# A transformer block with sliding-window attention on one core: another order for a batch's score products, the fifth block's projection in the attention's tail, and new tables of places

## The chip, the core and the metric

The kernel runs on one core of a Trainium2 chip. A core has a matrix engine (TensorE, PE in the profile; its weight loads are PEld), VectorE (DVE), ScalarE (ACT), GpSimd (POOL) and SyncE (SP, which here only issues DMAs). Each works through its own queue in order and waits for the others on semaphores. The metric is device time in microseconds (us).

## The reference

One transformer block over 2048 rows of 640, modulated by a vector c: layer norm, attention with 32 heads of 20 in which each row sees itself and the 255 rows before it, an output projection and a gated residual; then layer norm again and an MLP of width 1536.

```python
def A(x, wqkv, wo):                       # 32 heads of 20, W = 256
    q, k, v = split(x @ wqkv)
    scores = einsum("bhqd,bhkd->bhqk", q, k) * 20 ** -0.5
    mask = (i - j >= 0) & (i - j < 256)
    p = softmax(where(mask, scores, -1e9))
    return merge(einsum("bhqk,bhkd->bhqd", p, v)) @ wo

sa, ca, ga, sb, cb, gb = silu(c) @ w_mod  # six vectors of 640
h = layernorm(x) * (1 + ca) + sa
x = x + ga * A(h, wqkv, wo)
h = layernorm(x) * (1 + cb) + sb
x = x + gb * (gelu(layernorm(h) @ w1 + b1) @ w2 + b2)
```

## The kernel before

**Precision.** Every large product is made of three: an fp32 operand is split into a high part (a cast to fp32r) and a low part (the rest), and high x high, low x high and high x low are summed in PSUM. The names end in `hi` and `lo`. A cast of the high part is mostly ACT's; the low part, a subtraction, is DVE's or POOL's.

**Stages.** A prologue normalizes the first two chunks of 512 rows and makes the first q and k. Attention then runs in 139 steps (`t`). After it comes the MLP: four chunks of 512 rows, in each twelve slices `f` of the hidden width, with fifteen products into `h` and fifteen into `out` for each.

**The order is written out.** Every instruction goes through a helper (line 119, so that all rows of the profile bear L119) that keeps each engine's instructions in the program's order. What stands where is set by tables of numbers at the top of the file:

- The prologue is a string, `ORDER`, decoded letter by letter: R a warm run of small products, T a transposed column block of the normalized rows turned in, L its low part (on POOL if its name is in `LOWP`, else DVE), P the products with it, M a column of the modulation, S statistics, N the normalization, C, E, Y the layout of q and k. `RUN0` is the length of the first warm run.
- A step t of attention issues one batch of score products, the mask and exp of one item, the row maxima of another, and the sums with v of a third; behind them stand other tasks, at quarter steps, in `plan`. The q, k and v projections ("units") are laid into the steps up to `LAST` = 108 by `lay_units`, with a room of products for each step, corrected by `EXTRA`, `EARLY`, `AFTER`, `V_COST`, `X_COST` and others.
- The second half of the block is done for 16 blocks of 128 rows by `mid_steps(bg)`: load the sums `ob`, their scale `r` and the rows `xb`; scale them (`om`, on POOL), cast (`oh`, on ACT), subtract (`ol`, on POOL); thirty products with the output projection in two halves of 320 columns (`w00` to `w04`, `w10` to `w14`, three products each), both into one PSUM bank; an add and statistics for each half (DVE); the norm (`n1`, ACT), the modulation (`m0`, `m1`), transposes of the residual (`x0`, `x1`), the second norm (`n2`) and its transposes (`y0`, `y1`). Blocks 0 to 3 run in the last steps of attention, from the times `TAIL0` and with the offsets `TAIL_AT`. Of block 4 the loads and the scaling are there too; its other steps and blocks 5 to 15 (`mids`) are spread over the MLP by `fill()`, each chunk between `lo` and `hi`.

**A batch of score products.** `score_batch` issues the products of up to two groups: e (scores with k as rows, for exp; from step 11 on) and s (scores with q as rows, for the row maxima; until step 127). Each group holds four heads, two on PE's rows 0 to 63 and two on rows 64 to 127, and its scores lie in three PSUM banks of 512 columns. Letters name the products: `a` is the part of the first half that lies in the bank which both halves share, `b` and `c` the rest of the first half; `d`, `e` and `f` the same for the second half. A digit ahead of it is the group (0 for e, 1 for s). Since both halves must not write one bank at once, an empty instruction with a wait stands ahead of the second half's product into a shared bank. Each group has one set of banks, so that e of a step waits until exp has read the e before, and s until the maximum has read the s before.

Of the kernel before, what the change touches and what calls it, by code (L numbers as in the profile page):

```python
# [10 lines left out]
F32R = mybir.dt.float32r  # L11
# [21 lines left out]
RUN0 = 33  # L33
# [8 lines left out]
UNITS = (  # L42
    (0, "q1", "k1", "v0", "v1", "q2", "k2", "v2", "q3", "k3", "v30", "q40", "k40", "v40", "q41", "k41", "v31", "v41"),
    (1, "q00", "k00", "q10", "k10", "q01", "k01", "q11", "k11", "v0", "v1", "q2", "k2", "q3", "k3", "v2", "v3", "q4", "k4", "v4"),
)
FAST = 10
LNS = [-10.5, -3.5, -1.5, -1.5, 1.75, -1.0, 0.0]
LOV = [0, 1, 3, 4, 6, 7, 12, 17, 18, 21, 23, 24, 25, 26, 29, 40, 41, 42, 43, 46, 49, 50, 53, 56, 58, 60]
HIA = [0, 2, 6, 7, 9]
MV = [8, 9, 11, 12, 15, 19, 20, 21, 23, 27, 28]  # L50
# [10 lines left out]
EXTRA = {9: -2, 10: -2, 11: 6, 12: 1, 13: -1, 14: -2, 16: -4, 18: -3, 20: -5, 21: 4, 22: 6, 23: 3, 24: 1, 25: 4, 26: -1, 27: 5, 28: -4, 29: 1, 30: -4, 33: 4, 34: -3, 35: 2, 36: 3, 37: 3, 38: -6, 40: -2, 41: -1, 42: -3, 43: -3, 44: -7, 46: 2, 51: 1, 52: -8, 53: 6, 54: -8, 55: 2, 56: -3, 59: 8, 60: -2, 61: -1, 63: -1, 64: -4, 65: 3, 66: -4, 67: -2, 68: -2, 69: -2, 70: 1, 71: 3, 72: 4, 75: -1, 76: -2, 77: -3, 78: -2, 79: -3, 80: -3, 81: -9, 82: 16, 83: 6, 84: -2, 85: -1, 86: 2, 87: -2, 88: 3, 90: 2, 91: 1, 92: 3, 93: -7, 94: -10, 96: 8, 97: 1, 98: -1, 99: 5, 102: -2, 103: 6, 104: -4, 105: -2, 106: -1, 107: -2, 108: 1, 109: 1, 110: 3, 111: 7, 112: -1, 114: -1}  # L61

EARLY = {3: (5, 0, 0), 5: (3, 0, 0), 6: (3, 0, 0), 7: (3, 0, 0), 12: (1, 0, 0), 13: (0, 0, 0), 14: (0, 0, 0), 15: (5, 0, 0), 16: (5, 0, 0), 17: (4, 0, 0), 19: (4, 0, 0), 24: (4, 0, 0), 29: (3, 0, 0), 30: (5, 0, 0), 31: (2, 0, 0), 32: (0, 0, 0), 33: (3, 0, 0), 35: (5, 0, 0), 37: (5, 0, 0), 39: (4, 0, 0), 40: (4, 0, 0), 41: (3, 0, 0), 42: (4, 0, 0), 44: (2, 0, 0), 45: (0, 0, 0), 47: (5, 0, 0)}

AFTER = {2: 2, 3: 2, 4: 3, 5: 1, 6: 1, 7: 1, 9: 1, 10: 2, 11: 1, 12: 2, 14: 1, 15: 1, 19: 1, 20: 1, 22: 1, 23: 2, 25: 1, 32: 1, 35: 1, 40: 1, 41: 3, 43: 3}

SUMS_LAST = [14, 18, 25, 31, 32, 42, 43, 46, 50, 52, 55, 58, 60, 61, 62, 63, 76, 77, 78, 79, 88, 90, 91, 94, 95, 99, 101, 102, 103, 105, 108, 109, 110, 111, 115, 116, 117, 120, 122, 126, 127, 131, 132, 133, 136, 139]
LEAST = 4
MOST = 10
MODS = [[9.5, 17.0], [16.75, 27.5], [70.5, 79.0]]  # L70
WOS = [88.75, 91.75, 99.25, 110.25, 112.0, 113.25, 116.0]
W1S = [115.25, 121.0, 134.0]
RS = [[82.0, 82.5], [82.5, 86.75]]
TOMID = 110
WARM = {(130, 1): 2}
LATE_AT = [110.25, 110.5, 110.5, 111.5, 113.25, 114.25, 116.5]
TAIL0 = [115.25, 120.25, 124.25, 129.0, 138.25]
PER = 4.821
LATE = 0.8203
TAIL_AT = {'rd': -1.574, 'ri': -0.936, 'load': -0.924, 'om': -0.246, 'oh': 0.058, 'ol': 0.133, 'w00': 0.287, 'w01': 0.36, 'w02': 0.382, 'w03': 0.416, 'w04': 0.511, 'add0': 0.569, 'sa0': 0.649, 'w10': 0.71, 'w11': 0.711, 'w12': 0.722, 'w13': 0.83, 'w14': 0.865, 'add1': 0.885, 'sa1': 1.178, 'n1': 1.2, 'm0': 1.327, 'x0': 1.343, 'x1': 1.544, 'm1': 1.344, 'sb0': 1.505, 'sb1': 1.557, 'n2': 1.709, 'y0': 1.844, 'y0l': 1.92, 'y1': 2.026, 'y1l': 2.317}  # L80
# [44 lines left out]
def block_kernel(ctx: ExitStack, tc: tile.TileContext, x, wqkv, wo, w1, b1, w2, b2, c, crow, wmod, wcol, sel, outT):  # L125
# [425 lines left out]
    def score_batch(batches):  # L551

        cut = []
        for n, (t, parts) in enumerate(batches):
            cut.append([
                [(n, at // 512, t[:, at:to], lhs, rhs(off, to - at)) for col, size, lhs, rhs in part for at, to, off in cuts(slot, col, size)]  # L560
                for slot, part in enumerate(parts)
            ])
# [12 lines left out]
        for i, (half, mm) in enumerate(queue):
            n, bank, out, lhs, rhs = mm
            if half and (n, bank) in given:
                assert not [1 for h, m in queue[i:] if not h and m[:2] == (n, bank)]
                tc.add_manual_dep(
                    nc.tensor.nop().ins, given.pop((n, bank)).name, in_order, reason="rows of the array share a bank"  # L580
                )
# [240 lines left out]
    def mid_steps(bg):  # L822
# [84 lines left out]
        def ytrans(k0, k1):  # L907
            cs = slice(bl * P, (bl + 1) * P)

            def go():  # L910
                if not yT:
                    yT[0] = [base.tile([P, KT, CHUNK], F32R, tag=f"h{i}1", name=f"y{i}0") for i in ("hi", "lo")]
# [21 lines left out]
        times = TAIL_AT if bg < 4 else MID_AT  # L934
# [3 lines left out]
        at = lambda nm: times[nm[:2]] + 1e-6 if bg < 4 and nm in ("y0l", "y1l") else times[nm]  # L938
# [417 lines left out]
    yT[1] = [base.tile([P, KT, CHUNK], F32R, tag=f"h{i}0", name=f"y{i}1") for i in ("hi", "lo")]  # L1356
# [130 lines left out]
```

## Time and profile before

| | us |
|---|---|
| median of three runs | 1004.71 (1004.12 to 1005.11) |
| profiled execution | 1004.25 |
| its span, first to last instruction | 1002.5 |
| PE busy in it | 951.8 |
| first e batch | 98.73 |
| last e batch | 590.30 |
| first product of the MLP | 598.48 |

A row of the timeline gives the start (us from the start of the span), the duration, the engine, the line, the operation, the tile written and the tiles read (buffer numbers left out), and in brackets how long the engine had been idle and for what. A row of the waits says who waited for whom: the total, how many times, the longest. A row of a table by stage gives the stretch, its length, each engine's busy time (with its instructions) in the order PE, PEld, DVE, ACT, POOL, then the granted PE clock (1.00 is full speed), the share of time in which the DMA engines were busy, and GB/s.

### The profile page before, as it was taken

How to read it: one execution, taken by the hardware profiler on the slowest of the kernel's cores; microseconds unless marked ns; L12 is line 12 of the kernel's file. 1: busy time of each engine (PE TensorE's matmuls, PEld its weight loads, DVE VectorE, ACT ScalarE, POOL GpSimd, SP SyncE). 2: the span in 40 equal slices, each digit the busy share in tenths (PEclk: the TensorE clock that was granted, in tenths of full speed). 3: DMA queues.
4: the chain of work that ended last, by engine and by line, in shares of the span. 5: the costliest groups of instructions: out<-in, count | busy, mean ns of one | idle time of the engine just before them, and what ended most of it. 6: DMA issues, size and time to landing. Idle time of an engine off the chain costs nothing.

```text
span 1002.5 us, 19950 instructions
## 1 busy us (share of the span) xinstructions
PE 951.8 (95%) x7737; PEld 755.3 (75%) x7737; DVE 592.8 (59%) x939; ACT 444.6 (44%) x781; POOL 481.7 (48%) x680
## 2 busy tenths in 40 slices
PE   8899999999999999999698879999999999999997
PEld 7777777777777677777476658888888888888886
DVE  6564867879677787767678644765444444433112
ACT  3724545566654544554345663343433343333122
POOL 4423655676864354644537844454543445442221
PEclk9999999999999999999899989999999999999999
DMA  8265878557678269834662144444422334124113
GB/s 301 91 215 144 280 239 263 169 163 212 198 231 260 86 178 277 234 101 159 190 184 67 52 127 136 154 131 139 132 86 84 94 129 127 40 64 147 53 45 113
DMA packets 99262, 152.81 MB, mean 152 GB/s; under 512 B 8897, under 2 KB 42145, under 8 KB 99169
## 3 DMA queue, kind: packets, MB, share of 16 engines
q1 hardware_dynamic: 89952, 143.16, 46.3%
q10 hardware_dynamic: 9216, 8.39, 2.6%
q8 instruction: 61, 1.00, 0.4%
q14 instruction: 33, 0.26, 0.1%
HBM read 99.17 MB, written 51.58 MB: 150 GB/s over the span
## 4 chain that ended last, share of the span: by engine, by line
PE 80%; DVE 9%; ACT 4%; issue 2%; DMA 2%; POOL 1%; SPq 0%; DVEq 0%; ACTq 0%; POOLq 0%
PE pp L119 16%; PE out L119 16%; PE h L119 16%; PE o L119 7%; PE e L119 7%; PE wo L119 6%; PE s L119 6%; DVE e L119 3%; ACT pt L119 3%; DVE nm L119 2%; PE ppo L119 2%; DVE s L119 1%; PE yt L119 1%; PE pv L119 1%; PE xt L119 1%
## 5 line engine op out<-in xcount | busy, mean ns | idle before, releaser
L119 POOL TENSOR_SCALAR_AFFINE_SELECT pt<-pt 128x512 f32<-128x512 f32 x192 | 129.2, 673 | 149.3 <-ACT pt L119 142.6
L119 ACT ACTIVATE pt<-e 128x1024 f32<-128x1024 f32 (+1 forms) x120 | 133.6, 1114 | 66.6 <-DVE e L119 63.3
L119 POOL TENSOR_TENSOR w2lo<-w2r,w2hi 128x640 fp32r<-128x640 f32 x48 | 75.8, 1580 | 166.9 <-ACT w2hi L119 166.7
L119 DVE TENSOR_REDUCE nm<-s 128x4 f32<-128x1024 f32 (+1 forms) x128 | 152.7, 1193 | 4.4
L119 PEld LDWEIGHTS e<-qbuf,kbuf 62*128 62x128 f32 x773 | 81.5, 188 | 57.5 <-ACT pt L119 33.1
L119 PE MATMUL e<-qbuf,kbuf 62*128 62x128 f32 (+2 forms) x773 | 108.0, 320 | 17.3 <-ACT pt L119 17.0
L119 PE MATMUL s<-kbuf,qbuf 60*128 60x128 f32 (+2 forms) x728 | 108.3, 312 | 10.3 <-DVE nm L119 7.4
L119 PE MATMUL pp<-hhi,whi 128*128 128x512 f32 x265 | 114.0, 430 | 0.9 <-ACT whi L119 0.7
L119 DVE COPY_PREDICATED e<-mask_t,e 128x512 f32<-128x512 uint32 x96 | 66.6, 694 | 77.5 <-PE e L119 66.8
L119 DVE CAST ghi<-g 128x512 fp32r<-128x512 f32 x48 | 27.1, 565 | 143.9 <-ACT g L119 143.8
L119 PE MATMUL pp<-hlo,whi 128*128 128x512 f32 x265 | 107.6, 406 | 3.1 <-POOL hlo L119 3.1
L119 PE MATMUL pp<-hhi,wlo 128*128 128x512 f32 x265 | 108.2, 408 | 0.0
L119 PE MATMUL o<-pt,vbuf 128*32 128x128 f32 x2688 | 102.1, 282 | 0.5 <-ACT oT L119 0.4
L119 PEld LDWEIGHTS s<-kbuf,qbuf 60*128 60x128 f32 x728 | 82.9, 187 | 21.7 <-DVE nm L119 5.4
L119 POOL TENSOR_TENSOR wlo<-wraw,whi 128x128 fp32r<-128x128 f32 x180 | 77.9, 463 | 39.9 <-ACT whi L119 32.0
L119 PE MATMUL out<-ghi,w2hi 128*128 128x512 f32 x240 | 96.2, 401 | 0.0
L119 PE MATMUL h<-yhi,w1hi 128*128 128x512 f32 x240 | 95.8, 399 | 0.0
L119 PE MATMUL out<-ghi,w2lo 128*128 128x512 f32 x240 | 94.1, 392 | 0.0
L119 PE MATMUL out<-glo,w2hi 128*128 128x512 f32 x240 | 94.0, 392 | 0.0
L119 PE MATMUL h<-ylo,w1hi 128*128 128x512 f32 x240 | 93.9, 391 | 0.0
L119 PE MATMUL h<-yhi,w1lo 128*128 128x512 f32 x240 | 93.9, 391 | 0.0
L119 ACT COPY oT<-o 128x128 f32<-128x128 f32 x128 | 33.8, 264 | 128.2 <-PE o L119 121.8
(169 smaller groups left out, 1840.8 us busy)
## 6 DMA issues: line engine op xcount, KB each, us to landing
w2r<-in_w SPq DMA_DIRECT2D x48, 320.0 KB
qbuf<-q_scr SPq DMA_DIRECT2D x60, 240.0 KB
wraw<-in_wqkv SPq DMA_DIRECT2D x37, 320.0 KB
kbuf<-k_scr SPq DMA_DIRECT2D x44, 240.0 KB
q_scr<-stage SPq DMA_DIRECT2D x20, 512.0 KB
k_scr<-stage SPq DMA_DIRECT2D x20, 512.0 KB
o_scr<-oT ACTq DMA_DIRECT2D x64, 128.0 KB
wm<-in_wmod SPq DMA_DIRECT2D x20, 320.0 KB
```

What stands on the lines that cost most here:

```text
L119: return self.tc.keep_in_program_order(op(*args, **kw))
```

## The change

Three things change at once.

**The order of a batch's products.** `BOTH`, the order for a batch of two groups, is another one, and the code that puts in the waits for shared banks now does so in both directions (whichever half comes second in a bank waits for the last product of the first).

**The fifth block.** `TAIL0` loses its fifth entry. Block 4's steps whose time is under `CROSS` = 0.72 run in the tail from `NEXT` = 134.0: besides the loads and the scaling these are the cast, the low part, the five steps of the first half of the projection with its add and statistics, and two steps of the second half. Its remaining steps, the norms among them, are in the MLP, whose spreading starts at `LO0` = 4.6 in place of 4. The buffers of the second norm's transposes are made where they are first used.

**The tables.** `ORDER`, `LOWP`, `UNITS`, `LNS`, `LOV` (units whose evacuation is DVE's), `MV` (modulations that are DVE's), `EXTRA`, `EARLY`, `AFTER`, `SUMS_LAST` (steps in which exp goes ahead of the copies of the sums) and the times of the other tasks have new numbers.

```diff
-RUN0 = 33
+RUN0 = 37
-ORDER = ('T00 M1 L00 S0 S1 R12 S2 R3 S3 T01 M2 L01 P00 N T02 P01 M3 R3 T03 T10 L03 L02 M4 R1 T11 R1 R6 L10 C P02 T04 P10 L11 T12 P03 T13 L04 L13 P11 L12 P04 E0 T14 Y00 P12 P13 L14 Y01 P14')
-LOWP = ['L13', 'L10', 'L03', 'L01', 'L00', 'L14', 'L12']
+ORDER = ('T00 M1 L00 S0 S1 S2 R3 S3 T01 R12 L01 P00 N M2 T02 P01 M3 R3 T03 T10 L03 L02 T11 M4 R1 C L10 P02 T04 R6 P10 L11 T12 L04 P03 L12 T13 L13 P11 P04 E0 T14 Y00 P12 P13 L14 Y01 P14')
+LOWP = ['L10', 'L03', 'L00', 'L14', 'L13', 'L12']
...
-MV = [8, 9, 11, 12, 15, 19, 20, 21, 23, 27, 28]
+MV = [9, 12, 15, 19, 20, 21, 23, 26, 27]
...
-V_COST = 3.06
-X_COST = 1.84
+V_COST = 2.84
+X_COST = 1.79
 
 ONE = "0a 0d 0b 0e 0c 0f".split()
-BOTH = "0a 0d 0b 1a 1d 0e 0c 0f 1c 1e 1f 1b".split()
+BOTH = ['0f', '0c', '0d', '1a', '1b', '1d', '0b', '1e', '0a', '0e', '1c', '1f']
...
-TAIL0 = [115.25, 120.25, 124.25, 129.0, 138.25]
+TAIL0 = [115.25, 120.25, 124.25, 129.0]
+NEXT = 134.0
+CROSS = 0.72
+LO0 = 4.6
 PER = 4.821
-LATE = 0.8203
+LATE = 0.8152
...
-        given = {}
-        for i, (half, mm) in enumerate(queue):
-            n, bank, out, lhs, rhs = mm
-            if half and (n, bank) in given:
-                assert not [1 for h, m in queue[i:] if not h and m[:2] == (n, bank)]
-                tc.add_manual_dep(
-                    nc.tensor.nop().ins, given.pop((n, bank)).name, in_order, reason="rows of the array share a bank"
-                )
+        rest = collections.Counter((half, *mm[:2]) for half, mm in queue)
+        shares, given = rest.copy(), {}
+        for half, (n, bank, out, lhs, rhs) in queue:
+            other = given.pop((1 - half, n, bank), None)
+            if other is not None:
+                tc.add_manual_dep(nc.tensor.nop().ins, other.name, in_order, reason="rows of the array share a bank")
+            assert rest[1 - half, n, bank] in (0, shares[1 - half, n, bank])
             ins = matmul(out, lhs, rhs, start=True, stop=True).ins
-            if not half and bank in both[n]:
-                given[n, bank] = ins
-
+            rest[half, n, bank] -= 1
+            if not rest[half, n, bank] and rest[1 - half, n, bank]:
+                given[half, n, bank] = ins
...
-            eng = nc.vector if now[0] >= MODV and bg < 4 or 2 * bg + h in MV else nc.gpsimd
+            eng = nc.vector if now[0] >= MODV and bg < len(TAIL0) or 2 * bg + h in MV else nc.gpsimd
...
-            if bg > 3 and bg + time >= 4:
+            start = (TAIL0 + [NEXT])[min(bg, len(TAIL0))]
+            if bg >= len(TAIL0) and (bg > len(TAIL0) or time >= CROSS):
                 mids.append((bg + time, bg, go))
                 continue
-            tail.append((TAIL0[min(bg, 4)] + time * PER, nm, go))
+            tail.append((start + time * PER, nm, go))
...
-        lo, hi = (4, 9) if ch == 0 else (4 * ch + 5, 4 * ch + 9)
+        lo, hi = (LO0, 9) if ch == 0 else (4 * ch + 5, 4 * ch + 9)
```

How this moves instructions is shown at three places.

PE, an ordinary batch of two groups in the middle of attention (e of one item, s of another; each row is a product with the shapes of its rows and columns). Before:

```order
L119 MATMUL e0_2_3_1975<-qbuf2_98,kbuf2_101 128x256
L119 MATMUL e0_2_3_1975<-qbuf2_98,kbuf2_101 128x384
L119 MATMUL e0_2_3_1975<-qbuf2_98,kbuf2_101 128x128
L119 MATMUL s0_3_6_1976<-kbuf0_99,qbuf0_96 128x256
L119 MATMUL s0_3_6_1976<-kbuf0_99,qbuf0_96 128x384
L119 MATMUL e0_2_3_1975<-qbuf2_98,kbuf2_101 128x128
L119 MATMUL e0_2_3_1975<-qbuf2_98,kbuf2_101 128x384
L119 MATMUL e0_2_3_1975<-qbuf2_98,kbuf2_101 128x256
L119 MATMUL s0_3_6_1976<-kbuf0_99,qbuf0_96 128x384
L119 MATMUL s0_3_6_1976<-kbuf0_99,qbuf0_96 128x128
L119 MATMUL s0_3_6_1976<-kbuf0_99,qbuf0_96 128x256
L119 MATMUL s0_3_6_1976<-kbuf0_99,qbuf0_96 128x128
```

and now:

```order
L119 MATMUL e0_2_3_1978<-qbuf2_98,kbuf2_101 128x256
L119 MATMUL e0_2_3_1978<-qbuf2_98,kbuf2_101 128x384 x2
L119 MATMUL s0_3_6_1979<-kbuf0_99,qbuf0_96 128x256
L119 MATMUL s0_3_6_1979<-kbuf0_99,qbuf0_96 128x128
L119 MATMUL s0_3_6_1979<-kbuf0_99,qbuf0_96 128x384
L119 MATMUL e0_2_3_1978<-qbuf2_98,kbuf2_101 128x128
L119 MATMUL s0_3_6_1979<-kbuf0_99,qbuf0_96 128x128
L119 MATMUL e0_2_3_1978<-qbuf2_98,kbuf2_101 128x256
L119 MATMUL e0_2_3_1978<-qbuf2_98,kbuf2_101 128x128
L119 MATMUL s0_3_6_1979<-kbuf0_99,qbuf0_96 128x384
L119 MATMUL s0_3_6_1979<-kbuf0_99,qbuf0_96 128x256
```

The products are the same twelve. The e group now ends at the tenth place where it ended at the eighth, and 1024 columns of it, where there were 768, come ahead of the first s product.

POOL, in the last steps of attention (`pt1_7_n` are the exp tiles of the last items, whose edges POOL sets to zero; `rsa3`, `nra3` and `rsb3`, `nrb3` the two norms of block 3; `ob4` and `ot14` the scaled sums and the low part of block 4; `w2lo` weights of the MLP). Before:

```order
L119 AFFINE_SELECT pt1_7_3_7668<-pt1_7_3_7668 128x4x128 x2
L119 AFFINE_SELECT pt1_7_4_7706<-pt1_7_4_7706 128x4x128 x2
L119 AFFINE_SELECT pt1_7_5_7735<-pt1_7_5_7735 128x4x128 x2
L119 TENSOR_TENSOR rsa3_7743<-rsa3_7743,mhalf_68 128x1
L119 TENSOR_TENSOR nra3_7747<-mva3_7742,rsa3_7743 128x1
L119 TENSOR_SCALAR nra3_7747<-nra3_7747 128x1
L119 AFFINE_SELECT pt1_7_6_7772<-pt1_7_6_7772 128x4x128 x2
L119 TENSOR_TENSOR rsb3_7830<-rsb3_7830,mhalf_68 128x1
L119 TENSOR_TENSOR nrb3_7834<-mvb3_7829,rsb3_7830 128x1
L119 TENSOR_SCALAR nrb3_7834<-nrb3_7834 128x1
L119 TENSOR_TENSOR ob4_7787<-ob4_7787,r4_7789 128x640
L119 TENSOR_TENSOR w2lo0_0_7949<-w2r0_6654,w2hi0_0_7948 128x640
```

and now:

```order
L119 AFFINE_SELECT pt1_7_3_7655<-pt1_7_3_7655 128x4x128 x2
L119 TENSOR_TENSOR ob4_7570<-ob4_7570,r4_7572 128x640
L119 AFFINE_SELECT pt1_7_4_7693<-pt1_7_4_7693 128x4x128 x2
L119 TENSOR_TENSOR ot14_7703<-ob4_7570,ot04_7702 128x640
L119 AFFINE_SELECT pt1_7_5_7726<-pt1_7_5_7726 128x4x128 x2
L119 TENSOR_TENSOR rsa3_7734<-rsa3_7734,mhalf_68 128x1
L119 TENSOR_TENSOR nra3_7738<-mva3_7733,rsa3_7734 128x1
L119 TENSOR_SCALAR nra3_7738<-nra3_7738 128x1
L119 AFFINE_SELECT pt1_7_6_7763<-pt1_7_6_7763 128x4x128 x2
```

Block 4's two operations stand ahead of block 3's first norm; the low part came behind the first `w2lo` before. On PE, nine products of block 4's projection (`wo4`) now stand between block 3's transposes and the last e batch, six between two of the sums behind it, and six between the next two; nine are left in the MLP.

DVE, in the prologue, behind the statistics of chunk 1 (`rs1`, `nr1` its norm, `xs1` its rows, `sa`, `ca1` modulation columns, `hlo0` the low part of chunk 0). Before:

```order
L119 TENSOR_SCALAR rs1_265<-mv1_264 128x4
L119 COPY sa_77<-psm_150 128x1
L119 TENSOR_SCALAR ca1_78<-psm_150 128x1
L119 SCALAR_TENSOR_TENSOR nr1_322<-mv1_264,rs1_265 128x4
L119 TENSOR_SCALAR xs1_0_133<-xs1_0_133,mv1_264,rs1_265 128x640
L119 TENSOR_SCALAR xs1_2_135<-xs1_2_135,mv1_264,rs1_265 128x640
```

and now:

```order
L119 TENSOR_SCALAR rs1_269<-mv1_268 128x4
L119 TENSOR_TENSOR hlo0_251<-hf0_1_292,hhi0_250 128x512
L119 SCALAR_TENSOR_TENSOR nr1_314<-mv1_268,rs1_269 128x4
L119 TENSOR_SCALAR xs1_0_133<-xs1_0_133,mv1_268,rs1_269 128x640
L119 TENSOR_SCALAR xs1_2_135<-xs1_2_135,mv1_268,rs1_269 128x640
L119 COPY sa_77<-psm_150 128x1
```

The low part of chunk 0's second column block, which POOL made, is DVE's now and stands right behind `rs1`; the modulation columns follow later.

More of the change, by code (lines that the diff above doesn't have):

```diff
@@ L74 @@
+W1S = [115.0, 122.0, 133.75]
+RS = [[81.75, 82.5], [82.5, 88.75]]
 TOMID = 110
-WARM = {(130, 1): 2}
-LATE_AT = [110.25, 110.5, 110.5, 111.5, 113.25, 114.25, 116.5]
-TAIL0 = [115.25, 120.25, 124.25, 129.0, 138.25]
+WARM = {(130, 1): 3}
+LATE_AT = [110.25, 110.5, 110.75, 111.5, 113.75, 114.0, 116.5]
+TAIL0 = [115.25, 120.25, 124.25, 129.0]
+NEXT = 134.0
+CROSS = 0.72
+LO0 = 4.6
 PER = 4.821
-LATE = 0.8203
-TAIL_AT = {'rd': -1.574, 'ri': -0.936, 'load': -0.924, 'om': -0.246, 'oh': 0.058, 'ol': 0.133, 'w00': 0.287, 'w01': 0.36, 'w02': 0.382, 'w03': 0.416, 'w04': 0.511, 'add0': 0.569, 'sa0': 0.649, 'w10': 0.71, 'w11': 0.711, 'w12': 0.722, 'w13': 0.83, 'w14': 0.865, 'add1': 0.885, 'sa1': 1.178, 'n1': 1.2, 'm0': 1.327, 'x0': 1.343, 'x1': 1.544, 'm1': 1.344, 'sb0': 1.505, 'sb1': 1.557, 'n2': 1.709, 'y0': 1.844, 'y0l': 1.92, 'y1': 2.026, 'y1l': 2.317}
+LATE = 0.8152
@@ L81 @@
+TAIL_AT = {'rd': -1.372, 'ri': -1.024, 'load': -0.924, 'om': -0.246, 'oh': 0.058, 'ol': 0.133, 'w00': 0.287, 'w01': 0.36, 'w02': 0.382, 'w03': 0.416, 'w04': 0.511, 'add0': 0.569, 'sa0': 0.649, 'w10': 0.71, 'w11': 0.711, 'w12': 0.722, 'w13': 0.855, 'w14': 0.865, 'add1': 0.885, 'sa1': 1.178, 'n1': 1.2, 'm0': 1.327, 'x0': 1.343, 'x1': 1.544, 'm1': 1.344, 'sb0': 1.505, 'sb1': 1.557, 'n2': 1.683, 'y0': 1.844, 'y0l': 1.922, 'y1': 2.026, 'y1l': 2.38}
 MID_AT = {
@@ L910, in go @@
             def go():
-                if not yT:
-                    yT[0] = [base.tile([P, KT, CHUNK], F32R, tag=f"h{i}1", name=f"y{i}0") for i in ("hi", "lo")]
+                if ch < 2 and ch not in yT:
+                    yT[ch] = [base.tile([P, KT, CHUNK], F32R, tag=f"h{i}{1 - ch}", name=f"y{i}{ch}") for i in ("hi", "lo")]
                 bx["py", k0] = turned(bx["y"], f"yt{bg}", k0, k1)
@@ L933, in mid_steps @@
             steps["rd"], steps["ri"] = r_steps(ch)
-        times = TAIL_AT if bg < 4 else MID_AT
+        times = TAIL_AT if bg < len(TAIL0) else MID_AT
         for now_, then in CHAIN:
             assert times[now_] < times[then], (now_, then)
-        at = lambda nm: times[nm[:2]] + 1e-6 if bg < 4 and nm in ("y0l", "y1l") else times[nm]
+        at = lambda nm: times[nm[:2]] + 1e-6 if bg < len(TAIL0) and nm in ("y0l", "y1l") else times[nm]
         return [(at(nm), bg, nm, go) for nm, go in steps.items()]
```

24 lines of the change are left out of this document (9 added, 15 removed).

## The prediction

> **What bounds the kernel now.** I read first the page's busy shares and chain, then the waits of PE, then PE's busy time by stage, and last single stretches of the timeline.
>
> ```profile
> PE 951.8 (95%) x7737; PEld 755.3 (75%) x7737; DVE 592.8 (59%) x939; ACT 444.6 (44%) x781; POOL 481.7 (48%) x680
> PE 80%; DVE 9%; ACT 4%; issue 2%; DMA 2%; POOL 1%; SPq 0%; DVEq 0%; ACTq 0%; POOLq 0%
> PE e L119 <- ACT pt L119: 17.0, 23, 2.6
> PE s L119 <- DVE nm L119: 7.4, 14, 1.3
> PE pp L119 <- POOL hlo L119: 3.1, 1, 3.1
> PE wo L119 <- DVE xb L119: 1.2, 1, 1.2
> ...
> 98.73:474.13 375.40, 363.81 (x3991) 271.07 (x3990) 283.33 (x361) 202.38 (x379) 213.06 (x350) 1.00 0.67 204
> ...
> 558.35:598.48 40.13, 31.25 (x460) 22.35 (x459) 22.24 (x47) 23.86 (x42) 25.26 (x42) 0.91 0.26 74
> 598.48:1002.50 404.02, 397.06 (x1932) 335.25 (x1931) 167.63 (x303) 134.81 (x213) 163.28 (x169) 1.00 0.34 107
> ```
>
> PE sets the time (the waits' columns: total, times, longest): 95% busy, 80% of the chain. The last three rows are stages: length, then PE's busy time. The 97 steps from the first e batch to the end of the projections (t = 11 to 107, 98.73 to 474.13) take 375.40/97 = 3.87 us each with 11.6 us of PE idle in all; the MLP (from 598.48) idles 7 us in 404. So there only less PE time, or a shorter issue of the same products, can save. Of the 40 us before the MLP PE idles 9: work put there is nearly free, if it does not lengthen what PE waits for.
>
> **The change, part by part.**
>
> *Block 4.* In PE's queue, as the rows of the change above show, nine products of block 4 come ahead of the last score batch and twelve between the later sums; nine of its thirty stay in the MLP.
>
> ```profile
> 606.74 0.31 PE L119 MATMUL wo<-wo_hhi,ot 128*128 128x320 f32 x1
> 606.88 0.31 PE L119 MATMUL wo<-wo_hlo,ot 128*128 128x320 f32 x1
> ...
> 607.92 0.73 ACT L119 CAST w2hi<-w2r 128x640 fp32r<-128x640 f32 x1 [2.79 <-DMA w2r<-in_w]
> 608.73 1.57 POOL L119 TENSOR_TENSOR w2lo<-w2r,w2hi 128x640 fp32r<-128x640 f32 x1 [5.00 <-ACT w2hi L119]
> 611.77 0.41 PE L119 MATMUL wo<-wo_hhi,ot 128*128 128x320 f32 x1 [1.23 <-DVE xb L119]
> ```
>
> Start to start a product costs .147 us in the MLP: 21 leave, −3.1. PE's 1.23 us for the DVE add between block 4's halves (one PSUM bank for both) goes too: −1.2. Late next is block 5, which moves up: its POOL scaling and low part now stand behind the second w2lo, which cannot start before 608.73 since the weight lands at 607.9. So POOL scales block 5 from 610.3 to 611.9 (1.57, as w2lo), makes block 4's rsa and nra (1.2, from 587.06 to ACT's y at 588.25 in the next fence), and then the low part, to 614.6. The products that now stand ahead of block 5's first low product, at .23 and .147 from 598.48, bring PE there at 613.7: a new wait of .9, between 0 (PE late by another wait) and 2.5 (the weight later still). Sum for the MLP: −3.4.
>
> Block 4's three loads stood in the tail before as well; on SP's queue they only pass one store. Where its products and POOL's work go:
>
> ```profile
> 585.76 1.34 POOL L119 TENSOR_SCALAR_AFFINE_SELECT pt<-pt 128x512 f32<-128x512 f32 x2 [1.13 <-ACT pt L119]
> 587.06 0.57 POOL L119 TENSOR_TENSOR rsa<-rsa,mhalf 128x1 f32<-128x1 f32 x1
> 588.25 0.92 ACT L119 ACTIVATE y<-xb,nra,rsa 128x640 f32<-128x640 f32 x1 [2.40 <-POOL nra L119]
> 590.30 1.12 PE L119 MATMUL e<-qbuf,kbuf 62*128 62x256 f32 x8 [2.56 <-ACT pt L119]
> 591.54 1.54 DVE L119 COPY_PREDICATED_SCALAR e<-mask_t,negc 128x512 f32 x2
> 595.51 1.55 POOL L119 TENSOR_TENSOR ob<-ob,r 128x640 f32<-128x640 f32 x1
> 595.58 0.92 ACT L119 ACTIVATE y<-y,nrb,rsb 128x640 f32<-128x640 f32 x1 [0.50 <-POOL nrb L119]
> 596.58 0.55 PE L119 MATMUL yt<-idn,y 128*128 128x128 f32 x3
> ```
>
> The nine (1.3 us) fit in PE's 2.56 us before e1_7_7, the other twelve between sums that wait for ACT and DVE; costed at nothing on PE, since block 3's norm chain (POOL rsa, ACT y, DVE, ACT y, PE yt) ends last; without that cover, 3.1. But POOL's two 1.55 us operations, block 4's scaling and low part, now stand ahead of rsa in that chain, each between two selects. POOL idled 1.13 us before the 585.76 select; a 1.57 us low part in that gap pushes it by about .45, and rsa3 with ACT's y and all behind it: +.45. Below, 0 (if the chain has slack elsewhere); above, +2 (if ob4 delays the select before as well). The Trainium skill ("GPSIMD Engine Reference", 8. Key points) says that GpSimd shares its SBUF interfaces with VectorE and contends with two-input DVE instructions; by that the DVE masks and statistics beside ob4 and ot14 would lengthen too, a loss, and the sum would be some .5 higher. No row here separates it.
>
> *The order of a batch.* A batch holds the exp scores e of one item and the max scores s of another, on two row halves of PE.
>
> ```profile
> 300.47 0.39 PE L119 MATMUL pp<-hlo,whi 128*128 128x512 f32 x1
> 300.70 0.39 PE L119 MATMUL pp<-hhi,wlo 128*128 128x512 f32 x1
> 301.02 0.45 PE L119 MATMUL e<-qbuf,kbuf 62*128 62x256 f32 x3
> ...
> 302.07 0.43 PE L119 MATMUL o<-pt,vbuf 128*32 128x128 f32 x8
> ...
> 558.35 0.62 PE L119 MATMUL e<-qbuf,kbuf 62*128 62x384 f32 x4
> 558.90 0.32 PE L119 MATMUL o<-pt,vbuf 128*32 128x128 f32 x4
> ...
> 480.87 0.44 PE L119 MATMUL e<-qbuf,kbuf 62*128 62x256 f32 x2 [0.94 <-ACT pt L119]
> 484.35 0.45 PE L119 MATMUL e<-qbuf,kbuf 62*128 62x256 f32 x3 [0.94 <-ACT pt L119]
> 485.18 0.45 PE L119 MATMUL s<-kbuf,qbuf 60*128 60x256 f32 x2 [0.39 <-DVE nm L119]
> ```
>
> A batch that waits for nothing takes 302.07 − 301.02 = 1.05 us. A product of 512 columns takes .23 start to start, so .45 ns a column; 1536 columns on each half make .69. The e-only batch (768 a half, .35) takes .55, so entry and exit cost .20. Left: .16 lost inside the order. The old order has five places for it: three neighbours on the same half (0b 1a, 1d 0e, 1e 1f) and two where the second half enters a bank straight behind the first (0a 0d, 1a 1d). The new has one same-half pair (1a 1b) and one near entry (1d, two places behind 1a; 0a comes six behind 0d). Three of five places gone would be .10; I take half, .05, since the rows cannot price each. Bounds: −.16 and, if the added semaphore waits in the other direction cost as much as the places removed, +.10.
>
> Counted in PE's queue there are 109 batches of two groups; the waits name 23 + 14 stalls, so about 72 run unstalled: −3.6. In the 14 that wait for DVE, more e columns (1024, not 768) now precede s, so 256 columns over two halves (.06) are done during the wait: −.8. In the 23 that wait for ACT, the last e product ends 384 columns before the batch does instead of 448 a half, so the chain e, mask, exp, e gains .02: −.5. But a step that waits has a floor, 484.35 − 480.87 = 3.48 against the mean 3.87, and part of what unstalled steps win turns into the next step's wait: of −4.9 I count two thirds, −3.3.
>
> *The prologue.* The low part of column block 1 moves from POOL to DVE, ahead of nr, which waits for POOL's rs anyway.
>
> ```profile
> 23.66 0.17 DVE L119 TENSOR_SCALAR rs<-mv 128x4 f32<-128x4 f32 x1
> 24.95 1.26 POOL L119 TENSOR_TENSOR hlo<-hf,hhi 128x512 fp32r<-128x512 f32 x1
> 26.27 0.58 PE L119 MATMUL pp<-hlo,whi 128*128 128x512 f32 x1 [3.09 <-POOL hlo L119]
> 29.54 0.68 DVE L119 TENSOR_TENSOR hlo<-hf,hhi 128x512 fp32r<-128x512 f32 x1
> 30.49 0.78 ACT L119 ACTIVATE hf<-psx,sa,ca 128x512 f32<-128x512 f32 x1 [1.16 <-PE psx L119]
> ...
> 23.10:26.50 3.40, 0.31 (x2) 0.23 (x2) 2.19 (x7) 0.23 (x1) 2.24 (x2) 1.00 0.66 112
> 26.50:29.90 3.40, 3.40 (x13) 2.95 (x13) 3.37 (x22) 2.79 (x4) 0.00 (x0) 0.51 0.46 120
> ```
>
> On DVE it runs 23.8 to 24.5 and PE resumes 1.8 us sooner, perhaps without the half clock that followed the idle window (.31 busy, then .51 granted). What follows is held by ACT, which waits for PE 1.16 at 30.49. I take −.8, between 0 and −1.8.
>
> *The rest.* Two weight reloads and their casts vanish, some parts change between POOL and DVE, and product pieces move by one to three between steps without changing a count: 0, ±1, their cover being the queues that wait for PE.
>
> Sum: −3.4 + .45 − 3.3 − .8 = −7.05. The profiled execution took 1004.25 (its span 1002.5 and 1.75 around it) beside the median of 1004.71; from the median, **997.7 us**.
>
> **The rivals.**
>
> 1. *The order gains all that the five places say*: .10 in 109 batches, two thirds kept, −7.3 for −3.3: 993.7. For it: PE-bound steps have slack over the floor. Against: the floor, and a wait kept. The Trainium skill ("TensorE: Matmul & The Clock Gate", Part 3, What overlaps and what doesn't) says a weight load overlaps running products only where the row group differs; that speaks for this rival, with two fewer same-half loads. By it the two pairs would give up to a load each, twice the 188 ns of this row, which is more than a batch loses in all:
>
> ```profile
> L119 PEld LDWEIGHTS e<-qbuf,kbuf 62*128 62x128 f32 x773 | 81.5, 188 | 57.5 <-ACT pt L119 33.1
> ```
>
> So the loss of .16 caps it, and the chance stays low.
> 2. *Hidden anyway*: the order yields nothing (its loss sits at entry and exit), block 5's low part costs the full 2.5, leaving −1.8 in the MLP, the tail +.45 and the prologue 0: 1004.71 − 1.4 = 1003.3. For it: 37 stalls already; POOL is idle 5.00 us before w2lo, so the weight's landing, not PE, sets it.
> 3. *Slower, by bank handovers*: the old order ran every shared bank from first half to second; the new one goes from second to first for e (0d, then 0a), from first to second for s, and waits on a semaphore in both. At +.10 in 109 batches, two thirds felt, +7.3, with −3.75 of the other parts: 1008.3. It decides from .05 a batch (+3.7). For it: each wait costs PE a pause. Against: the old waits fell on the very next product, the new ones two and six places later.
>
> **How the numbers follow.** Forecast .57, rival 1 .17, rival 2 .15, rival 3 .11. The range: down to rival 1 (993.0 with a little of the clock), up past rival 2 to 1004.8, which leaves out rival 3 and the end of rival 1. A time within .2% (2.0 us) is about what a measurement cannot tell from no change: faster than 1002.7 are the forecast and rival 1, .74; within, rival 2 and a share of rival 3's small prices, .16; slower .10.
>
> **What would show it.** Unstalled batches of 1.00 us or less instead of 1.05; the mean step under 3.85; no wo wait for xb and 21 fewer wo products in an MLP of some 400.6 us; a wait for ot of up to 2.5; the last yt of block 3 some .45 later counted from the exp before; the wait for hlo near 1.3. I am wrong if batches are longer than 1.05, if e's waits for ACT grow beyond 20 us, or if the MLP does not shrink by at least 2.

## The result, and the profile after

| | median us (range, runs) | ratio to before, 95% interval |
|---|---|---|
| before | 1004.12 (1000.90 to 1005.11, 9) | |
| changed | 1000.14 (998.16 to 1002.49, 9) | 0.9969 (0.9956 to 0.9981) |

The change makes the kernel faster, by .31% or 3.1 us (1.9 to 4.4). The prediction said 997.7, 7.0 us or .70% faster: the sign is right, the size more than twice too large.

The page of the changed kernel, its span, busy shares and chain:

```profile
span 998.4 us, 19991 instructions
PE 955.0 (96%) x7745; PEld 753.3 (75%) x7745; DVE 593.0 (59%) x938; ACT 443.1 (44%) x777; POOL 479.4 (48%) x671
PE 78%; DVE 10%; ACT 5%; issue 3%; POOL 2%; DMA 2%; DVEq 0%; ACTq 0%; POOLq 0%
```

PE is about as busy as before (955.0 for 951.8) and still sets the time. PE's waits in the changed kernel (total, times, longest):

```profile
PE e L119 <- ACT pt L119: 14.4, 24, 1.6
PE s L119 <- DVE nm L119: 6.7, 13, 1.4
PE wo L119 <- POOL ot L119: 1.6, 2, 1.3
PE wo L119 <- DVE xb L119: 1.5, 2, 0.9
...
PE pp L119 <- DVE hlo L119: 1.3, 1, 1.3
```

The wait for the prologue's low part is 1.3 instead of 3.1, as predicted. The waits of a batch are as many as before (24 + 13 for 23 + 14); they are 3.3 us shorter in sum (14.4 + 6.7 for 17.0 + 7.4), 1.0 of it in one place, the wait ahead of the last e batch (1.58 for 2.56), which nine products of block 4 now fill in part. Two projection waits stand in the place of one.

The changed kernel by stage: to the first e batch, to t = 108, to t = 114, the last steps before the MLP, the MLP (length, then PE, PEld, DVE, ACT, POOL busy, granted PE clock, DMA share, GB/s):

```profile
0.00:97.48 97.48, 90.87 (x495) 73.68 (x496) 57.01 (x142) 42.71 (x75) 33.39 (x60) 0.98 0.56 187
97.48:474.18 376.70, 364.14 (x3990) 268.16 (x3990) 285.14 (x363) 200.97 (x377) 206.56 (x339) 1.00 0.67 202
474.18:500.14 25.96, 23.59 (x233) 16.22 (x233) 18.07 (x22) 11.34 (x21) 13.86 (x15) 0.67 0.69 195
...
556.51:596.88 40.37, 32.23 (x483) 23.96 (x482) 23.05 (x49) 24.55 (x43) 27.14 (x43) 1.00 0.26 74
596.88:998.40 401.52, 394.32 (x1911) 331.98 (x1909) 163.74 (x297) 134.48 (x212) 166.78 (x172) 1.00 0.35 107
```

and the stretch from t = 108 to t = 114 in the kernel before, whose limits were not shown there:

```profile
474.13:502.12 27.99, 19.55 (x233) 14.05 (x232) 18.09 (x22) 11.44 (x21) 13.86 (x15) 0.88 0.64 191
```

By stage the two profiles differ by −1.25 (prologue), +1.30 (t = 11 to 108, where most of the order's −3.3 was forecast), −2.03 (t = 108 to 114, where nothing of that size was), +.14 (t = 114 to 128), +.24 (last steps) and −2.5 (MLP), −4.1 in all. Two of these are not the change. Two other kernels have the instructions of the kernel before in the stretch 108 to 114, and took 26.4 (prologue_alone) and 26.7 (block4_alone) for 28.0, so it varies by 1.6 us by itself. And in the stretch 11 to 108 the changed kernel had one window of 3.4 us at half clock (.5 granted), at 188.5, that the kernel before had not; block4_alone, which has the old tables there, had it too (188.3) and took 376.68. One profile of each kernel cannot show an effect of 1 us; the table below adds more kernels and many timed runs.

### The profile page after: what moved, and what is told of

The parts are those of the page before. It is cut to its first block, busy times and chain, and to the rows that moved or that the text cites. A ratio compares the mean times of both kernels' runs of the same rounds, so it can differ in the third digit from the quotient of the medians.

```text
span 998.4 us, 19991 instructions
## 1 busy us (share of the span) xinstructions
PE 955.0 (96%) x7745; PEld 753.3 (75%) x7745; DVE 593.0 (59%) x938; ACT 443.1 (44%) x777; POOL 479.4 (48%) x671
## 3 DMA queue, kind: packets, MB, share of 16 engines
q8 instruction: 62, 1.02, 0.4%
## 4 chain that ended last, share of the span: by engine, by line
PE 78%; DVE 10%; ACT 5%; issue 3%; POOL 2%; DMA 2%; DVEq 0%; ACTq 0%; POOLq 0%
PE pp L119 16%; PE out L119 16%; PE h L119 15%; PE e L119 7%; PE o L119 6%; PE wo L119 6%; PE s L119 5%; DVE e L119 4%; ACT pt L119 3%; DVE nm L119 2%; PE ppo L119 2%; PE warm L119 1%; DVE s L119 1%; PE yt L119 1%; DMA w2r<-in_w 1%
## 5 line engine op out<-in xcount | busy, mean ns | idle before, releaser
L119 PE MATMUL e<-qbuf,kbuf 62*128 62x128 f32 (+2 forms) x773 | 114.4, 332 | 15.3 <-ACT pt L119 14.4
L119 PEld LDWEIGHTS e<-qbuf,kbuf 62*128 62x128 f32 x773 | 79.0, 189 | 56.0 <-ACT pt L119 31.9
L119 PE MATMUL s<-kbuf,qbuf 60*128 60x256 f32 (+2 forms) x728 | 106.8, 311 | 9.4 <-DVE nm L119 6.7
L119 POOL TENSOR_TENSOR wlo<-wraw,whi 128x128 fp32r<-128x128 f32 x170 | 73.6, 464 | 38.7 <-ACT whi L119 37.3
```

The costliest lines, as they stand in the source:

```text
L119: return self.tc.keep_in_program_order(op(*args, **kw))
```

## The experiments

Lengths come from one profile of each kernel: to the first e batch; from there to t = 108; from t = 128 to the MLP's first product; the MLP. "Batch" is the median over the batches of twelve products that waited for nothing, from the first e product to the first product behind the batch; "e ends" is the end of its last e product, counted from the same start (the profile models the ends of products).

| kernel | median us | ratio (95%) | to e | 11-108 | 128-MLP | MLP | batch | e ends |
|---|---|---|---|---|---|---|---|---|
| before | 1004.12 | | 98.73 | 375.40 | 40.13 | 404.06 | 1.048 | .887 |
| changed | 1000.14 | .9969 (.9956-.9981) | 97.48 | 376.70 | 40.37 | 401.51 | 1.024 | .907 |
| order_alone | 1002.04 | .9991 (.9979-1.0004) | 98.20 | 374.38 | 39.94 | 403.06 | 1.019 | .907 |
| after_old_order | 1000.47 | .9975 (.9963-.9987) | 97.07 | 375.59 | 40.37 | 401.77 | 1.046 | .886 |
| block4_alone | 1002.12 | 1.0000 (.9989-1.0010) | 98.14 | 376.68 | 40.36 | 402.30 | | |
| prologue_alone | 1001.97 | .9988 (.9978-.9998) | 98.20 | 375.81 | 40.74 | 404.23 | | |
| tables_alone | 1001.99 | .9999 (.9989-1.0009) | 98.59 | 375.28 | 40.61 | 402.60 | | |
| after_e_first | 1018.67 | 1.0163 (1.0144-1.0182) | 97.36 | 392.08 | 40.84 | 401.23 | 1.439 | .884 |
| after_e_early | 993.01 | .9908 (.9892-.9924) | 97.53 | 371.02 | 41.12 | 400.96 | 1.044 | .822 |
| after_e_late | 1003.03 | 1.0008 (.9996-1.0019) | 97.62 | 379.07 | 41.11 | 400.73 | 1.005 | 1.033 |
| after_ot5_dve | 999.56 | .9973 (.9961-.9985) | 97.56 | 375.56 | 41.28 | 402.06 | | |
| after_no_block4 | 1002.13 | 1.0002 (.9991-1.0013) | 97.52 | 375.25 | 39.96 | 403.70 | 1.020 | .907 |
| before_e_early | 996.37 | .9949 (.9931-.9966) | 98.15 | 370.73 | 40.09 | 403.26 | 1.044 | .825 |
| e_early_no_block4 | 994.96 | .9923 (.9904-.9942) | 97.39 | 371.13 | 40.66 | 402.52 | 1.044 | .824 |
| e_early_again | 992.17 | .9904 (.9884-.9923) | 97.25 | 371.07 | 41.09 | 401.28 | 1.045 | .824 |
| e_early_ot5 | 996.28 | .9941 (.9925-.9957) | 97.22 | 373.77 | 40.37 | 400.86 | 1.108 | .825 |

The kernels were timed in five groups, the kernel before anew in each: its median was 1004.12 beside the changed kernel, and 1002.92, 1002.53, 1002.93 and 1002.84 in the others. So the ratios are compared, not the medians. A difference of two ratios from different groups carries this spread too.

### The four parts of the change, one by one

order_alone takes the new `BOTH` and the code for the waits into the kernel before; after_old_order puts the old order into the changed kernel.

```diff
-BOTH = "0a 0d 0b 1a 1d 0e 0c 0f 1c 1e 1f 1b".split()
+BOTH = ['0f', '0c', '0d', '1a', '1b', '1d', '0b', '1e', '0a', '0e', '1c', '1f']
...
```

> The kernel before with the new order of a batch's products alone. By the prediction's step: 3.3 us faster than before (0.33%), with unstalled batches .05 shorter. By the rival read from the changed kernel's trace (an unstalled batch goes from 1.048 to 1.024 us, but e ends at .907 in place of .887 after its start): unstalled steps win .02 and steps whose chain runs over e lose .02 to .04, so within 1 us of before, and the stretch from the first e batch to t = 108 keeps its 375.4 us within 1.

> The changed kernel with the old order of a batch's products. If the order is worth 3.3 us there: about 1003.4 by the medians, as much as before. If it is worth nothing: the changed kernel's time, about 1000.1, within 1. If the new tables were fitted to the new order, it could be slower than both parts say by 1 to 3 us.

Alone the order gave −.9 us (−2.1 to +.4), in the changed kernel .9975 to .9969, −.6. Neither is clear of nothing, and both exclude the predicted 3.3. It does shorten a batch, by about half of what was forecast:

```profile
301.45 0.56 PE L119 MATMUL e<-qbuf,kbuf 62*128 62x256 f32 x3
...
302.47 0.64 PE L119 MATMUL o<-pt,vbuf 128*32 128x128 f32 x16
302.47 0.70 DVE L119 COPY_PREDICATED e<-mask_t,e 128x512 f32<-128x512 uint32 x1 [1.08 <-PE e L119]
```

This is the changed kernel's batch that answers to 301.02 before: 1.02 to the sums, not 1.05. But DVE's mask of e starts 1.02 after the batch's first product, where it started .99 after it (302.01 before).

block4_alone and after_no_block4 put block 4's first steps into the tail of the kernel before, and back into the MLP of the changed one.

```diff
-TAIL0 = [115.25, 120.25, 124.25, 129.0, 138.25]
+TAIL0 = [115.25, 120.25, 124.25, 129.0]
+NEXT = 134.0
+CROSS = 0.72
+LO0 = 4.6
...
```

> The kernel before with the fifth block's first steps in the tail alone. By the prediction: the MLP 3.4 us shorter (21 products and the wait for the add gone, a wait of .9 for block 5's low part come), its start .45 later: 3.0 faster. By the rival (what the changed kernel's trace shows: MLP 401.5 for 404.0 with waits for ot of 1.6 and for xb of 1.5): the MLP 2.5 shorter, so 2.1 faster.

> The changed kernel with block 4's first steps back in the MLP (start times, offsets and the spreading's start as before). By the prediction's step (-3.0): 3 us slower than the changed kernel, equal to before. By the trace's account (21 products -3.1, the wait for the add often short, a wait of 1.4 for block 5's low part and of .3 and .8 for DVE's adds come): 1 to 1.7 slower. By block4_alone as timed (0.0, -1.1 to +1.1): no difference, about 1000.1.

Timed, the move is worth 0.0 in the kernel before (−1.1 to +1.1) and 3.3 in the changed one (1.0002 against .9969). The profiles lie between, and closer together: with block 4 in the tail the MLP took 400.7 to 402.3 in nine profiles (mean 401.4), without it 402.5 to 404.2 in seven (mean 403.35), −1.9; the last steps took 40.77 against 40.30, +.47. That makes −1.5. A third pair, on the base of after_e_early, stands below.

prologue_alone and tables_alone take the new `RUN0`, `ORDER` and `LOWP`, and all other new tables, into the kernel before.

> The kernel before with the new order of the prologue alone. By the prediction: .8 faster, the wait for hlo 1.3 instead of 3.1. By the changed kernel's trace: the first batch 1.0 sooner, 1.0 faster in all. By the rival that later stages eat it: the first batch 1.0 sooner and no gain at t = 108.

> The kernel before with the new step tables alone (units, evacuations, rooms of the steps, times of the tail's tasks); old batch order, old prologue, block 4 in the MLP. By the prediction: nothing, within 1 us. By the rival that the gain of the changed kernel which its three named parts do not show (order -0.9, block 4 0.0, prologue -1.2 alone, -2.1 in all, against -3.1) is the tables': 1 us faster; if the tables serve only the new order or block 4, 0 to 1 us slower.

The prologue gave −1.2 (−2.2 to −.2). The tables gave nothing (−.1, −1.1 to +.9). In the profiles the first e batch stands at 98.36 in the mean of the five kernels with the old prologue, at 98.20 in prologue_alone, and at 97.40 in the mean of the ten that have the new prologue and the new tables: one profile of the prologue alone does not show the sooner first batch that both together have.

### What a batch's order is worth

The new order's batch is shorter and yet gains little. Three more orders in the changed kernel part the batch's length from the end of its e group: after_e_first, after_e_early and after_e_late, in this order.

```diff
-BOTH = ['0f', '0c', '0d', '1a', '1b', '1d', '0b', '1e', '0a', '0e', '1c', '1f']
+BOTH = "0a 0d 0b 0e 0c 0f 1a 1d 1b 1e 1c 1f".split()
+BOTH = "0f 0c 0d 0b 1a 1e 0a 0e 1d 1c 1f 1b".split()
+BOTH = "0f 0c 0d 1a 1b 1d 1c 0e 0a 1e 1f 0b".split()
```

> The changed kernel with a third batch order: all six products of e, then all six of s, the halves strictly alternating (0a 0d 0b 0e 0c 0f 1a 1d 1b 1e 1c 1f). No two neighbours lie on one half. If same-half neighbours cost the .16 that a batch loses, as the prediction had it: an unstalled batch falls from 1.024 to about .90. If waits for the bank that both halves share cost it (here the second half enters it five places behind the first, in place of eight): 1.02 or longer, about 1.1. By the theory that steps are bound by when e ends, e's end falls from .907 to about .7 in all steps and the kernel gains up to 3 us more even so.

> The changed kernel with a batch order in which e ends at its eighth place with s let in from the fifth, and one same-half pair early (0f 0c 0d 0b 1a 1e 0a 0e 1d 1c 1f 1b). If the chain e, mask, exp, e bounds steps: e's end .1 to .2 sooner, 1 to 3 us faster than the changed kernel. If the length of the batch bounds them: the same within 1 us.

> The changed kernel with a batch order that begins like the new one and is meant to be as long, but lets e end at the last place (0f 0c 0d 1a 1b 1d 1c 0e 0a 1e 1f 0b), by some .1 later. If the end of e decides (after_e_early: .085 sooner in an unstalled batch, .12 in a stalled one, for a batch .02 longer, and 7 us): 5 to 9 us slower than the changed kernel, so slower than the kernel before. If the length of the batch decides: within 1 us of the changed kernel.

after_e_first has no two neighbours on one half, and its batches are the longest. Its batch from 308.70 on:

```profile
308.70 0.89 PE L119 MATMUL e<-qbuf,kbuf 62*128 62x256 f32 x6
309.47 0.85 PE L119 MATMUL s<-kbuf,qbuf 60*128 60x256 f32 x6
309.69 0.69 DVE L119 COPY_PREDICATED e<-mask_t,e 128x512 f32<-128x512 uint32 x1 [1.49 <-PE e L119]
310.25 0.54 PE L119 MATMUL o<-pt,vbuf 128*32 128x128 f32 x12
```

It takes 1.55. The part of the second half that lies in the shared bank is `f`, not `d` (slots go by 384 columns over banks of 512, and `score_batch` gives the letter f to it); here it comes five places behind `a`, in the orders above the two lie seven or eight places apart. The median batch is .415 longer than the changed kernel's for two such closer handovers, about .2 each. The single records of the trace show where: the product that enters the shared bank second starts .53 us (e) and .50 (s) after the first, in the median of the batches that wait for nothing, and no product starts in the .2 us ahead of it. In the kernel before these are .54 and .51 as well, but there six other products fill the time. So an order without same-half neighbours is no gain, and a handover with too little between is dear.

after_e_early is the fastest order of the study, 9.2 us under before, though its batch is .02 longer than the changed kernel's; after_e_late, whose batch is the shortest of all (1.005), loses the whole gain. PE's busy time in the stretch 11 to 108 of after_no_block4 (the new order), after_e_early and after_e_late leaves it idle for 12.8, 10.5 and 16.2 us:

```profile
97.52:472.77 375.25, 362.48 (x3990) 267.10 (x3989) 284.48 (x363) 201.19 (x377) 207.13 (x339) 1.00 0.66 203
97.53:468.55 371.02, 360.57 (x3990) 266.49 (x3989) 283.41 (x363) 200.90 (x377) 207.59 (x339) 1.00 0.68 205
97.62:476.69 379.07, 362.89 (x3990) 268.67 (x3989) 284.68 (x363) 201.00 (x378) 206.88 (x339) 1.00 0.66 201
```

The steps from t = 114 to 128, which hardly differ from one profile to the next, tell the same: 56.2 us in five kernels with the old order, 56.4 in four with the new one, 55.0 to 55.1 in four with the early one and 57.7 in after_e_late (and in after_e_first, whose batch is the long one).

One item's batch, which waits for DVE's maxima ahead of s, in four kernels: the first e product, the first s product, DVE's mask of e, and the sums that follow the batch. The timeline of the kernel before:

```profile
322.17 0.44 PE L119 MATMUL e<-qbuf,kbuf 62*128 62x256 f32 x3
322.64 0.44 PE L119 MATMUL s<-kbuf,qbuf 60*128 60x256 f32 x2
...
323.43 0.70 DVE L119 COPY_PREDICATED e<-mask_t,e 128x512 f32<-128x512 uint32 x1 [0.93 <-PE e L119]
323.49 0.64 PE L119 MATMUL o<-pt,vbuf 128*32 128x128 f32 x16
```

The changed kernel:

```profile
323.08 0.55 PE L119 MATMUL e<-qbuf,kbuf 62*128 62x256 f32 x3
323.61 0.45 PE L119 MATMUL s<-kbuf,qbuf 60*128 60x256 f32 x3
...
324.41 0.64 PE L119 MATMUL o<-pt,vbuf 128*32 128x128 f32 x16
324.44 0.69 DVE L119 COPY_PREDICATED e<-mask_t,e 128x512 f32<-128x512 uint32 x1 [0.98 <-PE e L119]
```

after_e_early:

```profile
319.66 0.56 PE L119 MATMUL e<-qbuf,kbuf 62*128 62x256 f32 x4
320.08 0.35 PE L119 MATMUL s<-kbuf,qbuf 60*128 60x256 f32 x2
...
320.70 0.69 DVE L119 COPY_PREDICATED e<-mask_t,e 128x512 f32<-128x512 uint32 x1 [0.77 <-PE e L119]
320.80 0.64 PE L119 MATMUL o<-pt,vbuf 128*32 128x128 f32 x16
```

after_e_late:

```profile
323.83 0.56 PE L119 MATMUL e<-qbuf,kbuf 62*128 62x256 f32 x3
324.44 0.67 PE L119 MATMUL s<-kbuf,qbuf 60*128 60x256 f32 x4
...
325.22 0.64 PE L119 MATMUL o<-pt,vbuf 128*32 128x128 f32 x16
325.40 0.70 DVE L119 COPY_PREDICATED e<-mask_t,e 128x512 f32<-128x512 uint32 x1 [1.01 <-PE e L119]
```

From the first e product to the mask: 1.26, 1.36, 1.04, 1.57. This item parts the four more than most. In the median of all batches of twelve products it is 1.05, 1.07, .94 and 1.20 where s does not wait, and 1.52, 1.53, 1.44 and 1.61 where it does. The mask is DVE's first task of the step; exp waits for it, and DVE's mask of s and the maxima for the next s stand behind it in DVE's queue. An e product that stands behind a waiting s product in PE's queue waits with it. The new order has more e columns ahead of the first s product, but the other three e products all stand behind s products; in after_e_early four stand ahead of s and two behind two of s.

> The kernel before with the order of after_e_early alone. If the end of e decides whatever the tables are: 6 to 8 us faster than before (about .7%), and the other parts of the change are then worth what is left to after_e_early's 9.2 (.92%), 1.5 to 3 us. If the new tables are what lets it win: under 4 us faster.

On the kernel before, with the code for the waits, the early order gave −5.1 us (−6.9 to −3.4), so it does not need the new tables; with the other parts of the change it is .9908 and, timed again, .9904.

### Block 4 once more

after_ot5_dve gives block 5's low part to DVE; e_early_no_block4 and e_early_again are after_e_early without block 4 in the tail, and as it was; e_early_ot5 is after_e_early with that low part on DVE and `1b` ahead of `1f` at the batch's end.

```diff
-            nc.gpsimd.tensor_tensor(bx["oT"][1], bx["o"], f32(bx["oT"][0]), ALU.subtract)
+            (nc.vector if bg == 5 else nc.gpsimd).tensor_tensor(bx["oT"][1], bx["o"], f32(bx["oT"][0]), ALU.subtract)
```

> The changed kernel with block 5's low part on DVE instead of POOL, where it no longer stands behind block 4's rsa and nra. The trace of the changed kernel shows PE waiting 1.42 for it. If that wait is the price that eats block 4's gain: .7 to 1.4 of it goes, the MLP about 400.5 in place of 401.5. If the next wait (DVE's add, .3, or the weights) takes its place: MLP unchanged.

> The kernel of after_e_early with block 4's first steps back in the MLP, beside e_early_again on the same chip. By the account from seven profiles with block 4 in the tail and six without (MLP 401.5 for 403.5, tail 40.8 for 40.25): 1.5 slower than e_early_again. By block4_alone as timed: equal. By the difference of the changed kernel and after_no_block4: 3.3 slower.

> The kernel of after_e_early once more, as the partner of e_early_no_block4: .9% faster than before if its first timing (six runs) holds, .5% if the other base's (before_e_early) is the order's full worth and the rest of the change adds nothing.

> The kernel of after_e_early with block 5's low part on DVE and the last two products of a batch exchanged (the second half's entry into the shared bank of s comes last, one place later). If waits for block 5 set the MLP's first microseconds: up to .7 faster than e_early_again. If the exchange shortens the batch by its bank wait: up to 1 more. If DVE's own work takes the place: the same within 1 us.

The third pair gives .9923 against .9904, 1.9 us for block 4, and 1.5 by the spans of their profiles (993.6 and 992.1: 1.2 in the MLP less .4 in the last steps, the rest ahead of them). Its interval would also hold 0 and 3.3. So some 1.5 to 1.9 us is what the profiles and the mean of three timings (0.0, 3.3, 1.9) give. The first two timings' difference stays unexplained; after_no_block4 and the changed kernel were timed in different groups, the other two pairs beside one another.

The low part on DVE shortened its own wait (1.42 to about .67, in two gaps), but the next one, for DVE's add ahead of block 5's second half, grew from .3 to 1.5, and the MLP stayed (402.06, and 400.86 in e_early_ot5). The exchange of the last two products cost .06 a batch with the same end of e, and 2.7 us in the stretch 11 to 108: batches' length counts too. Here `1f` starts .49 us after `1a` in both orders; being the last product in one of them, it ends the batch later.

## Why the prediction was right in sign and wrong in size

**What bounds the kernel**: right in that PE sets the MLP. For attention it was incomplete: the steps that wait for nothing are bound by PE, but the place where e ends moves the time as well, at about the rate of the batch's length.

**The batch's order, −3.3**: this step failed. It divided the .16 that a batch loses over five places, taking `d` for the part in the shared bank, as the letters are explained above. In the kernel it is `f`, and `a` and `f` lie seven or eight places apart in both orders, so there was no entry straight behind the other half to win. A batch became .024 shorter, not .05. That the two pairs fewer gave this is not shown: after_e_late has two such pairs to the changed kernel's one, and a shorter batch. The rule of the Trainium skill ("TensorE: Matmul & The Clock Gate", Part 3, What overlaps and what doesn't), that a weight load overlaps running products only where the row group differs, speaks for fewer pairs. Here two fewer came with .024 and none at all with the longest batch (after_e_first).

And the step gave the waiting batches a gain of .02 by an earlier end of e; e ends .02 later where nothing waits, and where s waits the mask comes no sooner either (1.53 for 1.52). What the two effects are worth can be estimated from the stretch 11 to 108. By e_early_ot5, .063 in length is 2.7 us, so −.024 is about −1.0. By after_e_early against after_no_block4, −.085 in e's end and +.02 in length are −4.2, so −5.1 for e's end alone, and some +1.2 for +.02; by after_e_late (+.126 in e's end, −.015 in length, +3.8) it is only some +.7. The two effects about cancel by this estimate, and −.6 to −.9 was measured. Rival 3, a loss by handovers, is not what happened, but its mechanism is real: after_e_first shows it at .2 a handover.

**Block 4, −3.4 in the MLP and +.45 in the tail**: the mechanism was right, the size off. The products are gone (PE issues 339 in the MLP for 360), −3.1. The tail's +.45 came as +.47, in part by luck: counted from t = 128, block 3's rsa starts at 28.9 to 29.1 for 28.7 in every kernel with block 4 in the tail, and what else makes up the mean differs from profile to profile (in four of these nine the last e batch starts at 33.2 for 32.3). The lengthening that the prediction named with .5 did not come there: beside block 4's scaling and low part DVE's masks of e took .69 and its statistics .48 (.70 and .49 before). What was mis-sized are the waits of the MLP. The 1.2 us for DVE's add that one profile showed is not a fixed price: counted from start to start, less a product's own time, the stop there was 1.38, 1.38, .63, .36 and three times nothing in seven profiles with block 4 in the MLP, .5 in the mean. The timeline of tables_alone, PE at that place, has no gap:

```profile
609.67 0.39 PE L116 MATMUL out<-ghi,w2lo 128*128 128x512 f32 x1
609.89 0.30 PE L116 MATMUL wo<-wo_hhi,ot 128*128 128x320 f32 x1
```

The new wait for block 5's low part, taken as .9, was 1.42 (.7 to 1.5 in seven profiles, 1.3 in the mean). POOL in the changed kernel, and one operation of DVE:

```profile
608.59 1.74 POOL L119 TENSOR_TENSOR ob<-ob,r 128x640 f32<-128x640 f32 x1
608.95 1.93 DVE L119 TENSOR_TENSOR glo<-g,ghi 128x512 fp32r<-128x512 f32 x1
610.29 1.02 POOL L119 TENSOR_TENSOR rsa<-rsa,mhalf 128x1 f32<-128x1 f32 x1
...
611.86 1.54 POOL L119 TENSOR_TENSOR ot<-ob,ot 128x640 fp32r<-128x640 f32 x1
```

PE there, and at the later stop:

```profile
611.90 0.31 PE L119 MATMUL wo<-wo_hlo,ot 128*128 128x320 f32 x1
...
613.46 0.42 PE L119 MATMUL wo<-wo_hhi,ot 128*128 128x320 f32 x1 [1.25 <-POOL ot L119]
...
664.94 0.42 PE L119 MATMUL wo<-wo_hhi,ot 128*128 128x320 f32 x1 [0.66 <-DVE xb L119]
```

The place and the queue were as predicted, two POOL operations longer than taken (1.74 for 1.57, rsa 1.02 for .57). rsa is .57 at its other fifteen places; here it started while DVE's subtraction `glo` ran, and that one took 1.93 where its median is .69. It is not the whole of the wait: in after_old_order rsa took .57, the scaling waited .78 for its load of `r`, and the stop was 1.47. Not foreseen were two later stops for DVE's adds, .3 at 620.0 and .8 at 664.9, since all blocks behind block 4 move up and meet other work; a stop of .5 at the gate's products went. −3.1 − .5 + 1.3 + 1.1 − .5 = −1.7, beside the profiles' −1.9.

**The prologue, −.8**: right in the time (−1.2, −2.2 to −.2), and in its first step, as the changed kernel's timeline shows:

```profile
24.07 0.68 DVE L119 TENSOR_TENSOR hlo<-hf,hhi 128x512 fp32r<-128x512 f32 x1
...
24.81 0.79 PE L119 MATMUL pp<-hlo,whi 128*128 128x512 f32 x1 [1.30 <-DVE hlo L119]
```

PE resumes at 24.81 for 26.27. The half clock behind it did not vanish; it only starts at 24.6 for 26.6. The wait itself is no measure of the gain: in the four other kernels with the old prologue it was .5 to 1.7, with PE at half clock from 13.6 to 15.7 us on in place of 26.6. And how much of the 1.5 us reaches the first e batch without the new tables stays open, since prologue_alone has it at 98.20.

**The rest, 0**: right (−.1).

With the sizes measured the sum is −.7 − 1.5 − 1.2 − .1 = −3.5, beside −3.1 (−4.4 to −1.9). Rival 2 (hidden anyway) was right in its parts, an order that yields next to nothing and a wait that eats half of the MLP's gain, and wrong in giving the prologue nothing.

## What to carry to other kernels

In an in-order queue, the products whose result another engine waits for should stand ahead of those that may have to wait themselves; weigh this against the length of the batch, since here a microsecond of either, gained in every step, was worth about .4 to .6 us a step. Price a removed wait from several profiles, or from what sets its end: one of 1.2 us here was none in three profiles of kernels with the same products there. When work moves out of a stage, price what moves up behind it, with its own adds and low parts.

## What the runs showed of the hardware

The half-clock windows do not stand at fixed places: in the profiles the first began between 13.6 and 26.6 us, one at 188 appeared in two kernels of sixteen, and the one near 480 lasted from 6.8 to 20.5 us. The timed runs of the kernel before spread from 999.7 to 1005.1, .5%, with a mean clock between .979 and .995; twelve runs of a kernel beside 23 or 35 of the kernel before left intervals of about 1 us to each side.

Two row halves that write one PSUM bank in turn are dear when too little stands between: .2 us for each handover at five places' distance (after_e_first). In six orders the second entry came .46 to .58 us after the first (medians; .70 for e in after_e_late), whether four or seven other products stood between. So it seems that a handover costs what other products leave unfilled of some .5 us.

A POOL operation and a DVE subtraction of two operands, started one during the other, both took longer: rsa 1.02 for .57, `glo` 1.93 for .69.
